# A linear-attention and mixture-of-experts kernel: first 128 tokens as one block without state, first half sequence projected in fp32 from undivided operands

## The chip, the cores and the metric

The kernel runs on one core of a Trainium2 chip. The metric is the device time of one launch in microseconds (us). The kernel before takes 321.5 us (median of three runs, 321.44 to 322.52).

A core has five engines with queues of their own: TensorE (PE) multiplies matrices, with its weight loads shown as PEld; VectorE (DVE) and ScalarE (ACT) work elementwise and read its results; GpSimd (POOL) works elementwise; SyncE (SP) issues the DMAs here. Engines wait for each other by semaphores, and each works through its own queue in order.

## The reference

Two parts follow each other, for 4 sequences of 768 tokens. The first is a gated linear attention with 8 heads of 48 channels:

```
f = 1 / (1 + exp(-f_logit))
for t in range(768):
    state = f[t][:, None] * state + k[t] (outer) v[t]      # per head, 48 x 48
    y[t] = q[t] @ state
x = y of all heads side by side                            # 768 x 384 per sequence
```

The second is a mixture of 4 attention experts with width 64, causal, of which each token takes the best 2 by the logits `x @ w_gate`:

```
q, k, v = x @ wq[e], x @ wk[e], x @ wv[e]
a = softmax(causal(q @ k.T / 8))
out += (weight of e for the token, 0 if not in its top 2) * (a @ v @ wo[e])
```

## The kernel before, in words

**Windows.** The linear attention goes by windows of 128 tokens (`gla_window`), six for each sequence, 24 in all. A window loads f, k, q (names `fkq`) and v. ScalarE makes the logs of the gates, VectorE sums them up along the tokens (a scan, into `c`, L441), ScalarE exponentiates the sums both ways (L447, L448), and VectorE multiplies k by the one (L451) and q by the other (L452). TensorE transposes k (L460), so that it can form the growth of the state, k times v, for each half window of 64 tokens (L485). VectorE adds that to the state (`mid` after the first half, `state` after the second, L501, L504, L506). The scores k times q are made for the two 64-token halves apart (L554), and what a half takes from tokens before it comes from the state (L544). VectorE copies the scores under a causal mask (`copy_predicated`, into `xs`, L564), TensorE multiplies them by v (L579), and the result goes into `x`.

The products on fp32 data in the second part are made from halves: a value is rounded to a reduced form (fp32r), the rest is a second number, and three products (high by high, high by low, low by high: L645, L646, L647 in `mm3`) stand for one. So x has a high half (L295) and a low half (L613), and so have the weights (`weights`: load L372, high L376 or L295, low L381).

**Filling of x.** TensorE works on 128 rows in this kernel, and 8 heads of 48 are three times 128: heads 6 and 7 are spread over spare rows by six small DMAs in each group (`fill`, L300). Window 0 is an exception (`whole`): its products write all 128 rows at once, with the tiles `vz` and `mz` that hold the spread columns of v and of the state.

**Units.** The second part goes by units of half a sequence (384 tokens), eight in all. A unit projects q and k (`proj_qk`, names `qs` and `kk`) and v with the gate logits (`proj_v`, `vv` and `lg`), ranks the logits (`gate`), and for each expert makes scores, maxima (L799, L803), exponentials (L814), divides (L842, L297), transposes (L860), multiplies by v (L890) and by wo. Unit 0 is projected in pieces of 128 tokens, as each of the first three windows is done; the others in pieces of 384.

**Order.** A table of numbers (`SEQUENCE`) names every step in the order in which it is emitted, and a plus behind a number picks another of the engines that can do it. What stands earlier on an engine is done earlier there. A planner (`Order.run`) walks the table to place filler products: products on zeros (`zb`, L274) that keep TensorE busy where the planner expects it to wait; `SURE`, `EARLY` and `LANDS` are numbers of that planner. Weight blocks are loaded into a buffer (`stage`) that is later used for probabilities.

Of the kernel before, what the change touches and what calls it, by code (L numbers as in the profile page):

```python
# [7 lines left out]
F32 = mybir.dt.float32  # L8
# [11 lines left out]
E, HD = 4, 64  # L20
# [22 lines left out]
SURE, EARLY = 1.6, 17.6e3  # L43
# [13 lines left out]
LANDS = (1300, 3.7, 500, 900)  # L57

IN_TURN = ("x", "xs", "qs", "kk", "vv", "lg", "zz", "pt0", "pt1")
# [90 lines left out]
"""  # L150


# [1030 lines left out]
```

## Time and profile before

| | |
|---|---|
| median of 3 runs | 321.5 us |
| profiled execution, device time | 321.65 us |
| its span in the profile | 319.9 us |
| TensorE busy | 304.7 us (95%) |
| VectorE busy | 263.4 us (82%) |
| ScalarE busy | 224.5 us (70%) |
| GpSimd busy | 52.4 us (16%) |
| instructions | 12988 |

The profile is of one execution. Its times count from the start of the span. A product's busy time reaches from its start to the modelled end of its passage, so that neighbours overlap: how fast products follow each other is read from the distance of their starts. A fp32 product appears as two records.

### The profile page before, as it was taken

To read this page: it belongs to the slowest core of one execution; us is meant where nothing else is said; L and a number is where in the kernel's file an instruction comes from. 1 tells how busy PE (TensorE), PEld (TensorE's weight loads), DVE (VectorE), ACT (ScalarE), POOL (GpSimd) and SP (SyncE) were. 2 spreads that over 40 slices of the span, in tenths; PEclk is the share of its full clock that TensorE was granted. 3 is DMA by queue.
4 is the path that set the end of the run, shared out by engine and by line. 5 is a ranking of instruction groups with operands and counts; after the bars stand their busy time and mean duration, and the time that the engine had idled before them with its cause. 6 is when DMAs were issued, how large, how long until landed. Compare 5 with 4: busy or idle time off the path is not lost.

```text
span 319.9 us, 12988 instructions
## 1 busy us (share of the span) xinstructions
PE 304.7 (95%) x5495; PEld 251.9 (79%) x5495; DVE 263.4 (82%) x676; ACT 224.5 (70%) x584; POOL 52.4 (16%) x94
## 2 busy tenths in 40 slices
PE   8989998899999999999999999999998999999992
PEld 3669987698898966998889796888887786997771
DVE  5768889989998986898999996999977794889730
ACT  6546668687978796667988866578977662677740
POOL 6111002110242122010133150000010020102300
PEclk9999999999999999999999999999999999999998
DMA  7955653615404405532613405446300003001202
GB/s 196 240 135 163 160 165 88 178 50 171 96 3 115 130 13 141 160 94 54 184 51 115 114 4 151 139 115 180 95 4 2 28 2 77 11 28 51 76 1 84
DMA packets 14561, 30.90 MB, mean 97 GB/s; under 512 B 2240, under 2 KB 10752, under 8 KB 14496
## 3 DMA queue, kind: packets, MB, share of 16 engines
q1 hardware_dynamic: 14496, 30.00, 33.6%
q8 instruction: 45, 0.74, 1.0%
q14 instruction: 20, 0.16, 0.2%
HBM read 23.01 MB, written 4.72 MB: 87 GB/s over the span
## 4 chain that ended last, share of the span: by engine, by line
PE 60%; DVE 22%; ACT 9%; DMA 3%; issue 3%; SPq 1%; POOL 1%; ACTq 0%; POOLq 0%
PE mm L645 9%; PE mm L890 7%; PE mm L647 7%; PE mm L646 7%; PE sps L782 7%; PE mm L860 5%; PE mm L274 3%; ACT pp L814 3%; DVE nm L799 3%; PE sps L554 3%; PE sps L579 3%; DVE c L441 2%; DVE nm L803 2%; PE mm L485 2%; DVE xs L564 2%
## 5 line engine op out<-in xcount | busy, mean ns | idle before, releaser
L814 ACT ACTIVATE pp<-sps,nm 128x128 f32<-128x128 f32 (+5 forms) x96 | 60.2, 633 | 17.0 <-DVE nm L803 12.1
L842 POOL TENSOR_SCALAR pp<-pp,den,one 128x768 f32<-128x768 f32 (+5 forms) x46 | 38.6, 845 | 149.3 <-DVE den L823 84.0
L295 ACT ACTIVATE pt<-mm 128x384 f32<-128x384 f32 (+4 forms) x94 | 39.0, 450 | 13.9 <-PE mm L860 13.4
L782 PE MATMUL sps<-kk,qs 64*128 64x384 f32 (+4 forms) x384 | 43.4, 340 | 1.3 <-ACT pp L814 1.2
L645 PE MATMUL mm<-x,wqk 128*128 128x384 f32 (+1 forms) x120 | 40.2, 335 | 0.0
L890 PE MATMUL mm<-pt,vv 128*64 128x384 f32 (+2 forms) x304 | 39.3, 406 | 0.1
L646 PE MATMUL mm<-x,wqk 128*128 128x384 f32 (+1 forms) x120 | 38.3, 319 | 0.0
L647 PE MATMUL mm<-x,wqk 128*128 128x384 f32 (+1 forms) x120 | 38.3, 319 | 0.0
L860 PE MATMUL mm<-ident,pp 64*128 64x64 f32 x672 | 34.5, 231 | 1.9 <-POOL pp L842 0.8
L860 PEld LDWEIGHTS mm<-ident,pp 64*128 64x128 f32 x672 | 27.0, 139 | 9.4 <-issue 3.3
L890 PEld LDWEIGHTS mm<-pt,vv 128*64 128x64 f32 x304 | 20.3, 137 | 16.9 <-issue 12.7
L441 DVE TENSOR_TENSOR_SCAN c<-keep,fkq 112x512 f32<-112x512 f32 x24 | 29.5, 1229 | 5.0 <-ACT fkq L436 4.8
L782 PEld LDWEIGHTS sps<-kk,qs 64*128 64x128 f32 x384 | 31.1, 187 | 2.7 <-ACT pp L814 1.5
L803 DVE TENSOR_REDUCE nm<-sps 128x2 f32<-128x768 f32 (+3 forms) x32 | 25.6, 816 | 6.0 <-PE sps L787 4.5
L799 DVE TENSOR_REDUCE nm<-sps 128x1 f32<-128x640 f32 (+1 forms) x32 | 27.4, 884 | 3.4 <-PE sps L787 3.3
L645 PEld LDWEIGHTS mm<-x,wqk 128*128 128x128 f32 x120 | 22.6, 188 | 1.8 <-ACT pt L295 0.2
L645 PE MATMUL mm<-wvg,x 128*128 128x260 f32 x72 | 22.0, 306 | 1.3 <-DMA x<-x 1.3
L647 PEld LDWEIGHTS mm<-x,wqk 128*128 128x128 f32 x120 | 22.7, 189 | 0.0
L646 PEld LDWEIGHTS mm<-x,wqk 128*128 128x128 f32 x120 | 22.7, 189 | 0.0
L445 POOL TENSOR_SCALAR cmax<-c 112x4 f32<-112x4 f32 x24 | 6.7, 281 | 95.3 <-DVE c L441 94.2
L297 ACT ACTIVATE pp<-pp,den 128x256 f32<-128x256 f32 (+5 forms) x31 | 19.6, 638 | 3.1 <-DVE den L823 3.0
L646 PE MATMUL mm<-wvg,x 128*128 128x260 f32 x72 | 20.4, 283 | 0.0
(127 smaller groups left out, 728.9 us busy)
## 6 DMA issues: line engine op xcount, KB each, us to landing
fkq<-fkq SPq DMA_DIRECT2D x21, 672.0 KB, 5.2
v<-v SPq DMA_DIRECT2D x24, 200.0 KB, 5.2
out<-o SPq DMA_DIRECT2D x24, 192.0 KB, 2.6
fkq<-fkq SPq DMA_DIRECT2D x9, 224.0 KB, 6.7
x<-x SPq DMA_DIRECT2D x42, 48.0 KB, 2.5
pt<-wqk SPq DMA_DIRECT2D x3, 256.0 KB, 6.2
pt<-wvg SPq DMA_DIRECT2D x3, 130.0 KB, 4.8
pt<-wo SPq DMA_DIRECT2D x2, 192.0 KB, 3.7
```

The source lines that it names most:

```text
L295: nc.scalar.activation(out, in_, AF.Copy)
L441: nc.vector.tensor_tensor_scan(cb.t.rearrange("r p t -> r (p t)"), self.keep.rearrange("r p t -> r (p t)"), part(0).rearrange("r p t -> r ...
L645: nc.tensor.matmul(ps, lh, rh, start=first, stop=False)
L646: nc.tensor.matmul(ps, lh, rl, start=False, stop=False)
L647: nc.tensor.matmul(ps, ll, rh, start=False, stop=last)
L782: nc.tensor.matmul(out, qs.t[r, lq, tq], kk.t[r, lk, s0:s1], start=x == 0, stop=x == 2 and not diag)
L799: ms = [o.add("max", [("V", dcopy(n))], lambda _, j=j, n=n: nc.vector.tensor_reduce(nm.t[:, 0, j:j + 1], banks[j].t[:, :, :n // 2], axis=A ...
L803: ms = [o.add("max", [("V", dcopy(2 * n))], lambda _, x=x, c0=c0, n=n: nc.vector.tensor_reduce(nm.t[:, x], banks[0].t[:, :, c0:c0 + n], ax ...
L814: nc.scalar.activation(out, in_, AF.Exp, bias=nm.t[:, x, j:j + 1], accum_out=den.t[:, x, j:j + 1])
L842: nc.gpsimd.tensor_scalar(p, p, by, self.one, op0=ALU.mult, op1=ALU.mult)
L860: nc.tensor.transpose(tp.t[:, c:c + 64], pp.t[r, c0 + k * 128:c0 + k * 128 + 128], self.ident[r, r])
L890: nc.tensor.matmul(z.t[64 * j:64 * j + 64, a - p0:p1 - p0], ts[sb // TH]["vv"].t[:, sb % TH, e * HD:(e + 1) * HD], pt.t[:, sb, j, a:p1], s ...
```

## The change

The first window is done as one block of 128 tokens with no state: the scores of all 128 tokens with each other are made (the block of the second half against the first by eight more products), masked into a zeroed triangle (`tri`, in a buffer that later holds probabilities), and multiplied by v in 128 columns. The state products for this window, the zeroing products (`wipe`) and the tile `mz` go. The state itself is still formed, for the next window.

The first three windows write x undivided, in fp32, and the first unit's q, k, v and gate logits are one fp32 product each instead of three (`plain`), from the weights as they were loaded (`raw`). The split weights are needed from unit 1 on. The gate logits stay in the tile of v. The table is another one, and so are the planner's numbers.

```diff
-SURE, EARLY = 1.6, 17.6e3
+SURE, EARLY = 0.0, 0.0
-LANDS = (1300, 3.7, 500, 900)
+LANDS = (1300, 4.1, 300, 300)
 SEQUENCE = """
-0 18 4 35 39 5 61 1 7 9 40 2 3 36 6 67 68 8 37 62 11 12 13 14 42 10 15 63 38 16 20+ 69 44 19+ 17 71 21 46 22 72 41
+19 0 35 66 1 4 2 39 5 3 60 6 7 9 8 10 11 20 70 12 13 40 14 37 36 38 67 22 21 222 42 44 15 57 41 69 63 46 16 18+ 17
...
         if whole:
-            def wipe(e):
-                for c in range(2):
-                    nc.tensor.matmul(ab.t[:, c, NP * C:], self.zb[:, 0:128], self.zb[:, 0:NP * C], start=True, stop=True)
...
+            blank = o.add("st", [("P", 1150)], lambda e: nc.gpsimd.memset(tri(), 0.0), alloc=[full])
...
-            inter(1)
-        t = o.add("a", [("PE", 850 if whole else 760 if w else 747)], scores, [k1, q1, sm, sdone] + ([clear, zm] if whole else []),
+            if not whole:
+                inter(1)
+                return
+            for p in range(NP):
+                for j in range(2):
+                    a = (NP + p) * C
+                    nc.tensor.matmul(ab.t[0:64, 1 - j, a:a + C], part(1)[64 * j:64 * j + 48, p, 0:C],
+                                     part(2)[64 * j:64 * j + 48, p, C:W], start=True, stop=True)
+        t = o.add("a", [("PE", 930 if whole else 760 if w else 747)], scores, [k1, q1] + ([] if whole else [sm, sdone]),
...
         if whole:
+            sel = [o.add("gev", [("V", dcopy(512))], lambda e, k=k, r=slice(64 * k, 64 * k + 64): pred(
+                tri()[r, :, :, k], r, ab.t[r, :, 0:NP * C], self.below[r]), [t, blank], uses=[ab, full]) for k in range(2)]
+            sel.append(o.add("gev", [("A", acopy(512))], lambda e: self.copy(
+                e, tri()[0:64, :, :, 1], ab.t[0:64, :, NP * C:].rearrange("s c (p t) -> s c p t", t=C)), [t, blank], uses=[ab, full]))
...
+            if n < 3:
+                self.windows[n] = o.add("x", [("A", acopy(k)), ("V", dcopy(k))], lambda e: self.copy(
+                    e, xout(0).bitcast(F32), yin()), [y], uses=[ys if whole else ab, x])
...
+                    if plain:
+                        nc.tensor.matmul(ps.t[:, :n], self.raw(1, i)[:, ws], x.t[:, 0, i, cs].bitcast(F32), start=i == 0,
+                                         stop=i == 2)
+                        continue
...
-                        self.proj_qk(o, t, pr, x, a, e, need + wqk)
+                        self.proj_qk(o, t, pr, x, a, e, need + ql, plain=True)
                     for k in ws:
-                        self.proj_v(o, t, x, k, need + wvg)
+                        self.proj_v(o, t, x, k, need + vl, plain=True)
...
-                need += self.fill(o, x, 0, HALF, need)
+                need += self.fill(o, x, 0, HALF, need) + (wqk + wvg if u == 1 else [])
```

What the new table does to the engines' queues is shown at three places. The first is SP's queue from its start, before. `fkq ... 112x512` is one of f, k and q of a window (224 KB), `112x1536` all three (672 KB), `v` 200 KB, `pt_143<-wqk` a block of the q and k weights (256 KB), `pt_143<-wvg` one of the value and gate weights (130 KB). The loads of windows 0 to 2 come singly; the first two are f of windows 0 and 1, and k and q of window 0 come behind the weight block.

```order
L423 DMA fkq<-fkq 112x512 x2
L372 DMA pt_143<-wqk 128x512
L423 DMA fkq<-fkq 112x512 x2
L430 DMA v<-v 128x400
L423 DMA fkq<-fkq 112x512 x4
L430 DMA v<-v 128x400
L423 DMA fkq<-fkq 112x512
L372 DMA pt_143<-wqk 128x512 x2
L430 DMA v<-v 128x400
L428 DMA fkq<-fkq 112x1536
L372 DMA pt_143<-wvg 128x260 x2
```

And now (the names are the same but for the buffer's number):

```order
L432 DMA fkq<-fkq 112x512 x5
L439 DMA v<-v 128x400
L375 DMA pt_146<-wqk 128x512
L432 DMA fkq<-fkq 112x512 x2
L439 DMA v<-v 128x400
L432 DMA fkq<-fkq 112x512
L437 DMA fkq<-fkq 112x1536
L375 DMA pt_146<-wqk 128x512
L439 DMA v<-v 128x400
L375 DMA pt_146<-wqk 128x512
L432 DMA fkq<-fkq 112x512
L375 DMA pt_146<-wvg 128x260 x3
```

The first five loads are now f of windows 0, 1 and 2 and then k and q of window 0. The whole load of window 3 has moved ahead of two weight blocks and of the queries of window 2.

The second place is VectorE's queue, from the key product of window 0 to the masked copy of window 1's scores, before. L451 and L452 are the key and query products, L441 the scan (in the program a `SCALAR_TENSOR_TENSOR`), L564 the masked copy of scores, L613 the low half of x, L381 the low half of weights.

```order
L451 TENSOR_TENSOR fkq<-fkq 112x512
L441 SCALAR_TENSOR_TENSOR c<-keep,fkq 112x512
L452 TENSOR_TENSOR fkq<-fkq,c 112x512
L381 TENSOR_TENSOR wqk<-pt_143,wqk 128x512
L504 TENSOR_TENSOR state<-mm,mid 112x208
...
L506 TENSOR_TENSOR state<-state,c 112x192
L564 COPY_PREDICATED xs_93<-below,sps 128x512
...
L501 TENSOR_TENSOR mid<-mm,state 112x208
...
L613 TENSOR_TENSOR x<-sps,x 128x2x3x64
L564 COPY_PREDICATED xs_94<-below,sps 128x512
```

And now, over the same stretch (L460, L461: the products; L450: the scan; L572: the masked copy; L295: an eviction of transposed keys):

```order
L460 TENSOR_TENSOR fkq<-fkq 112x512
L461 TENSOR_TENSOR fkq<-fkq,c 112x512
L450 SCALAR_TENSOR_TENSOR c<-keep,fkq 112x512
L572 COPY_PREDICATED pt_128<-below,sps 64x8x64 x2
...
L513 TENSOR_TENSOR state<-mm,mid 112x208
L515 TENSOR_TENSOR state<-state,c 112x192
L295 COPY kt<-mm 128x4x64
...
L510 TENSOR_TENSOR mid<-mm,state 112x208
...
L572 COPY_PREDICATED xs_94<-below,sps 128x512
```

The query product stands ahead of the scan, the masked copy is two copies of 64 rows, no split of weights and no low half of x stands in the stretch, and an eviction has come from ScalarE.

The third place is TensorE's queue around window 0's scores, before. L274 are fillers, L554 the scores, L544 and L539 the state's part.

```order
L485 MATMUL mm<-v,kt 48x64
L274 LDWEIGHTS zb
L274 MATMUL sps<-zb 128x256
...
L554 MATMUL sps<-fkq 64x64 x16
L544 MATMUL sps<-fkq,mid 48x64 x3
L539 MATMUL sps<-fkq,mz 64x64 x3
```

And now (L469: transposes of keys; L556 and L565: scores, the second of the new block; L494: state growth):

```order
L469 MATMUL mm<-ident,fkq 128x48
L278 LDWEIGHTS zb
L278 MATMUL sps<-zb 128x512
L556 MATMUL sps<-fkq 64x64 x16
L565 MATMUL sps<-fkq 64x64 x8
L494 MATMUL mm<-v,kt 64x48
```

The scores of window 0 stand ahead of its state growth instead of behind it, and nothing of the state is multiplied for them.

## Rows read from the trace of the kernel before

**Rows 1.** Page, busy time of each engine: us, share of the span, instructions.
```profile
PE 304.7 (95%) x5495; PEld 251.9 (79%) x5495; DVE 263.4 (82%) x676; ACT 224.5 (70%) x584; POOL 52.4 (16%) x94
```

**Rows 2.** Page, chain that ended last, shares of the span by engine.
```profile
PE 60%; DVE 22%; ACT 9%; DMA 3%; issue 3%; SPq 1%; POOL 1%; ACTq 0%; POOLq 0%
```

**Rows 3.** Stages: us, each engine's busy us (instructions), clock, DMA share, GB/s.
```profile
8.00:14.00 6.00, 6.00 (x106) 3.62 (x104) 4.12 (x7) 2.98 (x9) 1.16 (x1) 1.00 1.06 259
16.00:18.00 2.00, 2.00 (x67) 1.64 (x65) 0.55 (x1) 1.12 (x2) 1.14 (x2) 1.00 0.00 0
24.33:45.75 21.42, 21.36 (x503) 19.97 (x501) 18.22 (x43) 13.95 (x35) 1.37 (x5) 1.00 0.54 154
45.75:80.00 34.25, 31.25 (x709) 26.94 (x709) 31.87 (x88) 26.22 (x80) 4.35 (x10) 1.00 0.45 128
80.00:300.00 220.00, 216.41 (x3776) 182.31 (x3776) 191.00 (x500) 163.61 (x424) 37.06 (x53) 1.00 0.29 80
```

**Rows 4.** Chain in order of time, 0 to 50 us: start, us, what.
```profile
1.87 7.96 PE mm L274 x25
...
13.01 0.62 PE sps L554 x32
...
19.98 0.75 DVE xs L564
...
21.58 0.62 PE sps L579 x29
...
23.00 0.72 issue
23.72 0.68 PE mm L485 x25
24.40 0.26 PE mm L645
...
38.06 4.98 DMA fkq<-fkq
...
44.84 1.23 DVE c L441
...
48.08 1.20 DVE nm L803 x2
```

**Rows 5.** Timeline of VectorE, 0 to 26 us: start, us, instruction [idle before].
```profile
7.87 0.69 DVE L451 TENSOR_TENSOR fkq<-fkq 112x512 f32<-112x512 f32 x1 [1.49 <-DMA fkq<-fkq]
...
12.73 0.68 DVE L451 TENSOR_TENSOR fkq<-fkq 112x512 f32<-112x512 f32 x1
...
18.11 0.38 DVE L501 TENSOR_TENSOR mid<-mm,state 112x208 f32<-112x208 f32 x1 [1.56 <-PE mm L485]
...
19.00 0.55 DVE L613 TENSOR_TENSOR x<-sps,x 128x384 fp32r<-128x384 f32 x1
...
20.88 1.34 DVE L381 TENSOR_TENSOR wqk<-pt,wqk 128x512 fp32r<-128x512 f32 x2
```

**Rows 6.** Timeline of TensorE's weight loads, 6 to 10 us.
```profile
6.79 2.55 PEld L274 LDWEIGHTS <-zb 128*128 128x128 bf16 x12 [0.28 <-issue]
```

**Rows 7.** Groups by line and shape: count | busy us, mean ns | idle before.
```profile
L645 PE MATMUL mm<-x,wqk 128*128 128x128 f32 x36 | 10.2, 284 | 0.0
...
L646 PEld LDWEIGHTS mm<-x,wqk 128*128 128x128 f32 x120 | 22.7, 189 | 0.0
```

**Rows 8.** Timeline of TensorE around 24.5 and 42.6 us.
```profile
24.49 0.28 PE L646 MATMUL mm<-x,wqk 128*128 128x128 f32 x1
24.60 0.28 PE L647 MATMUL mm<-x,wqk 128*128 128x128 f32 x1
...
42.55 0.28 PE L647 MATMUL mm<-wvg,x 128*128 128x260 f32 x1
42.67 0.29 PE L645 MATMUL mm<-wvg,x 128*128 128x260 f32 x1
```

**Rows 9.** Chain: probabilities times values of a second-half unit.
```profile
301.03 3.38 PE mm L890 x24
```

More of the change, by code (lines that the diff above doesn't have):

```diff
@@ L219, in run @@
                         t.clear = at
+            for b in t.uses if e in "VA" else ():
+                if b.psum and "VA"[e == "V"] in b.read:
+                    o = "VA"[e == "V"]
+                    start = max(start, b.read[o] + SEEN[o][e])
             start = max(start, free[e] + (leave if e == "PE" and t.modes[0] != mode else 0.0))
@@ L244, in run @@
                 b.left -= 1
+                b.read[e] = t.done
                 for k in b.free_at:
@@ L363, in weights @@
                          (self.wo, self.wo_d, E // 2, DM))[which]
-        last = []
+        last, loads = [], []
         for i in range(n):
@@ L383, in weights, with raw @@
             t = o.add("wl", [("S", 470)], load, alloc=[st], size=cols / 2)
+            loads.append(t)
             t = o.add("w", [("P", 160 + 0.833 * cols), ("A", acopy(cols) + 30)], hi, [t], uses=[st])
             last.append(o.add("w", [("V", dcopy(cols))], lo, [t], uses=[st], port=True))
-        return last
+        return last, loads
+    def raw(self, which, i):
+        a, cols = ((0, 260), (780, 512))[which]
+        return self.raws.t.rearrange("s k q t -> s (k q t)")[:, a + i * cols:a + (i + 1) * cols]
     def gla_pools(self, ctx):
@@ L536, in inter @@
                     g = j ^ (p // 2)
-                    if whole and c and p == 3:
-                        for i in range(3):
-                            nc.tensor.matmul(yo(i, g, c, 64), self.mz[64 * j:64 * j + 48, i],
-                                             part(2)[64 * j:64 * j + 48, p, c * C:c * C + C],
-                                             start=False, stop=cross == 0, skip_group_check=True)
-                    elif w or c:
+                    if w or c:
                         st, m = mid if c else old, outer(g)
@@ L545, in inter @@
                                          part(2)[64 * j:64 * j + 48, p, c * C:c * C + C],
-                                         start=cross == 1 and (g, c) not in begun and not whole, stop=cross == 0, skip_group_check=True)
+                                         start=cross == 1 and (g, c) not in begun, stop=cross == 0, skip_group_check=True)
                         begun.add((g, c))
@@ new lines, in gla_window @@
+            sel.append(o.add("gev", [("A", acopy(512))], lambda e: self.copy(
+                e, tri()[0:64, :, :, 1], ab.t[0:64, :, NP * C:].rearrange("s c (p t) -> s c p t", t=C)), [t, blank], uses=[ab, full]))
+        else:
+            sel = [o.add("gev", [("V", dcopy(512))], lambda e: pred(xsb.t, slice(0, 128), ab.t[:, :, 0:NP * C], self.below),
+                         [t], alloc=[xsb], uses=[ab])]
+        def outputs(e):
+            if whole:
+                for p in range(NP - 1):
+                    for q in (NP - 1, p):
+                        for g in range(2):
+                            v0, m = (2 * p + g) * D, 64 if q > p else 48
+                            nc.tensor.matmul(ys.t[64 * g:64 * g + m, p * W:p * W + W],
+                                             self.vz[:, g, p] if q > p else vb.t[:, v0:v0 + m],
+                                             tri()[:, 1 - (g ^ (q // 2)), q], start=q > p, stop=q == p,
+                                             skip_group_check=True)
+                return
@@ L589, in xout @@
         def xout(h):
-            return x.t[0:rows, h, 0:np_, oc].rearrange("r p (c t) -> r c p t", c=2)
+            out = x.t[0:rows, h, 0:np_, oc]
+            return out if whole else out.rearrange("r p (c t) -> r c p t", c=2)
         def yin():
-            return ab.t[0:rows, :, NP * C:(NP + np_) * C].rearrange("r c (p t) -> r c p t", p=np_)
+            if whole:
+                return ys.t[:, 0:np_ * W].rearrange("r (p t) -> r p t", p=np_)
+            return ab.t[:112, :, NP * C:].rearrange("r c (p t) -> r c p t", p=np_)
         place = o.place
@@ L604, in go @@
                     more(e)
-            y = o.add("y", [("PE", 760 + 310 * whole + cost)], go, [sel, lv] + ([zv] if whole else []) + list(needs),
-                      alloc=alloc,
-                      uses=[xsb, vb, fkq, x, mid, ab] + ([old] if w else []) + list(uses), modes=("q", "q"), edge=(0, 92))
-            y.spare, y.free = lambda: [ab.t[0:112, i, NP * C:] for i in range(0 if w else 1, 2)], t
-            k = np_ * W
+            y = o.add("y", [("PE", 1290 if whole else 760 + cost)], go, sel + [lv] + ([zv] if whole else []) + list(needs),
+                      alloc=list(alloc) + ([ys] if whole else []),
+                      uses=[vb, x] + ([full] if whole else [xsb, fkq, mid, ab]) + ([old] if w else []) + list(uses),
+                      modes=("c", "c") if whole else ("q", "q"), edge=(60, 100) if whole else (0, 92))
+            if not whole:
+                y.spare, y.free = lambda: [ab.t[0:112, i, NP * C:] for i in range(0 if w else 1, 2)], t
+            k = np_ * W
+            if n < 3:
+                self.windows[n] = o.add("x", [("A", acopy(k)), ("V", dcopy(k))], lambda e: self.copy(
+                    e, xout(0).bitcast(F32), yin()), [y], uses=[ys if whole else ab, x])
+                o.place = here
+                return y
             hi = o.add("x", [("A", acopy(k)), ("V", dcopy(k))], lambda e: self.copy(e, xout(0), yin()),
-                       [y], uses=[ab, x])
+                       [y], uses=[ys if whole else ab, x])
             self.windows[n] = o.add("x", [("V", dcopy(k))], lambda e: nc.vector.tensor_sub(xout(1), yin(), xout(0)),
-                                    [hi], uses=[ab, x])
+                                    [hi], uses=[ys if whole else ab, x])
             o.place = here
@@ L620, in gla_window, with fill @@
         return state[:2] + (None, finish)
-    def fill(self, o, x, a, b, needs):
+    def fill(self, o, x, a, b, needs, halves=2):
         out = []
@@ L629, in go @@
                 def go(e, i=i, r=r):
-                    self.move(x.t[r + 48:r + 64, :, i, a:b], x.t[r + 16 * i:r + 16 * i + 16, :, 3, a:b])
-                out.append(o.add("fill", [("S", 640)], go, needs, uses=[x], size=(b - a) / 8))
+                    self.move(x.t[r + 48:r + 64, 0:halves, i, a:b], x.t[r + 16 * i:r + 16 * i + 16, 0:halves, 3, a:b])
+                out.append(o.add("fill", [("S", 640)], go, needs, uses=[x], size=(b - a) / 16 * halves))
         return out
@@ L1072, in plan @@
                     o.place = 12.0 + 4 * k
[L1073 removed]
+                    fills[k] = self.fill(o, x, 128 * k, 128 * k + 128, [windows[k]], 1) if k else []
                 for a, e, ws in ((0, 128, (0,)), (128, 256, (1,)), (256, 384, (2,))):
```

86 lines of the change are left out of this document (41 added, 45 removed), and 107 rows, old and new, of the table SEQUENCE.

## The prediction

> **What bounds the kernel now.** First the page's table of engines: TensorE is busy for 95% of the span and VectorE for 82% [rows 1]. The chain that ended last is not TensorE alone, since 22% of it lies on VectorE [rows 2]. So I cut the span into stages [rows 3]. From 24.33 to 45.75 us, where the first half sequence is projected while the attention windows 3 to 5 are computed between, TensorE works 21.36 of 21.42 us and VectorE 18.22. From 45.75 to 80 TensorE has gaps of 3.0 us in 34.25 and VectorE works 31.87: there VectorE is as near to being the bound. From 80 to 300 TensorE is busy for 98%. What is saved before 45.75 is therefore kept, if the stages behind it start earlier by as much and get no more work.
>
> Before 24.33 nothing is full: TensorE's 22.07 us are partly the filler products on zeros (25 of them in one run of 7.96 us [rows 4]). This is a chain of waits, and the chain of work in order of time shows it [rows 4]: scores of window 0 at 13.01, the masked copy of window 1's scores at 19.98, its output products at 21.58, the last state product at 23.72, and the first projection at 24.40. Behind it VectorE's timeline [rows 5]: the key product of window 0 waits for its DMA until 7.87, that of window 1 comes at 12.73, the low half of x of window 0 at 19.00 and two low halves of weights end at 22.22. Meanwhile the DMA engines moved nothing from 16 to 18 us [rows 3], because the fourth window's load stood at the head of SP's queue and waited for a buffer.
>
> **The head, step by step.** Times are my estimates, laid out by hand from the durations in the rows.
> 1. Window 0's keys are still the fourth load: f of window 2 (224 KB) has taken the place of a weight block (256 KB) ahead of them. So the key product stays at 7.8 (0.69 long). The filler ahead of the transposes shrinks from two short products and 25 to 21; late ones are 0.21 apart (twelve in 2.55 [rows 6]), so TensorE is free at about 8.5 and the transposes start at 8.7, not after the 1.3 us of filler that now lies between.
> 2. Scores of window 0 no longer need the state, its two copies, or the wiping products: they wait for two VectorE products alone. The query product now stands ahead of the scan: 7.8 + two of 0.65 = 9.1, scores from 9.3 to 10.3 (24 products, where 16 take 0.62). Today 13.01 to 13.63.
> 3. Scan of window 1 (1.23 [rows 4]) to 10.4; then two masked copies of 64 rows at 0.75 each, since a copy's time goes by columns, not rows: to 11.9. That is one copy more than before.
> 4. Window 1's keys: with them 2024 KB are queued, 1096 more than with window 0's keys today, which landed at 7.87. At the 259 KB/us of the stretch from 8 to 14 us [rows 3] that is 4.2 us later: about 12.0. Its key product runs 12.0 to 12.7, today 12.73 to 13.41.
> 5. Behind it on VectorE: a scan (1.2), two products (1.3), an eviction and three state operations (0.3 to 0.4 each), the wait for ScalarE's exponential (0.5): window 1's masked copy at about 17.5, today 19.98. The low half of x (0.55), one masked copy and the wait for a state sum that stands before 18.11 [rows 5] are what goes.
> 6. Output products of window 1 at 18.4, today 21.58; last state product at 19.4, today 23.72 (before it stood 0.72 us of a stall of TensorE's own [rows 4], which I let go); first projection at 20.2, today 24.40: **4.2 us**.
>
> The projection's other inputs are in time: it needs raw weights, not split ones, so it waits for a DMA alone. By the same count the last of the three q and k blocks, 3832 KB into the queue, lands at 7.87 + 2904 / 259 = 19.1, give or take 1. This is the tightest point: if it slips past 20.2, each us costs one.
>
> **The projections of the first half.** Removed: 36 products of 128 columns, three times [rows 7], 0.11 apart [rows 8]: 108 x 0.111 = 12.0 us; and 27 of 260 columns, 0.12 apart with switching 0.13: 3.5. Added: 36 fp32 products of 128 columns and 9 of 260. The nearest fp32 row is the product of probabilities and values [rows 9]: 1920 columns for two column halves at once (four times 384, 256, 128) in 3.38, or 1.76 ns per column. That gives 0.225 and 0.458 each: 8.1 + 4.1 = 12.2. **Saving 3.3 us**, and all of it in a stage where TensorE is full. Bounds: if a tenth of the row is start-up (an estimate), 1.6 ns per column and 11.1; if every product also had to wait for two weight loads at 0.11 each, 45 x 0.22 = 9.9 more, 22.1. I take 12.2, as the row is the same kind of product.
>
> A rule of the Trainium skill speaks against this part (FP8 and Floating Point Precision, section TensorE Precision Notes): true fp32 is four passes through the array, where three products of the reduced form are three. By that ratio the projections would take 15.5 x 4/3 = 20.7 instead of 12.2 and the whole 323.2. The trace disagrees for 128 columns: reduced products of 128 columns follow each other as slowly (0.11) as nearly those of 260 (0.12) [rows 8], so half of their time is not columns, and the fp32 row has no such share. For 260 columns the two come out alike: 0.458 against 0.37.
>
> **Smaller things.** The low halves of x for three windows (0.55 for the first [rows 5], the others a little longer) go, about 1.8 us of VectorE; the small copies of gate logits, which join the evictions of values, I count as nothing. Against that, two splits of the q and k weights (0.67 each [rows 5]) and three of the value weights (half as wide, so 0.35) move from before 45.75 into or past the experts' start, where VectorE is near the bound. The blanking of the triangle (1024 columns) is on GpSimd, idle there. The fill DMAs keep their number (0.6 us of SP each) and halve their bytes, nothing on the path. I charge **0.6 us** for VectorE's displaced work, between 0 and 1.5.
>
> **Is it kept?** The chain today passes the load of window 6: issued 38.06, scan 44.84, first maxima 48.1 [rows 4]. It is issued when window 3's outputs are done; four fifths of the way from the first projection to the first scores, which takes 21.4 us today and, less the saving up to there (nine of the twelve q and k products and all of v: 2.5), 18.9: near 32.2, and the scan near 39. VectorE's list from window 2's query product (near 21) to the first maxima adds up to some 18.5 us by the durations above, so 40 without a wait, 41 to 42 with. Both gain 6 to 7 us: neither takes the place of TensorE's gain.
>
> **Sum.** The profiled execution took 321.65, of which the span is 319.9; the median is 321.5. 321.65 - 4.2 - 3.3 + 0.6 = 314.75; against the median 314.6. I say **314.7**, own range 312.3 to 317.3. The rest of the order table is redone too; where the order says the same work, I give it no gain or loss, and 1.5 us either way in that range.
>
> **Rivals.**
> - *Weight loads are not hidden (slower).* Place: TensorE from 20 to 40 us, all 45 fp32 products. An fp32 product with 128 stationary columns does not appear in this trace; rows 9 load 64. If both loads lay bare, 22.1 replaces 15.5: +6.6, less 4.2 of the head, and the displaced 0.6: 324.6. It decides from a mean of 0.44 us per product: (15.5 + 4.2) / 45. Against it: the reduced products come 0.11 apart although a load takes 0.19 [rows 7, 8], so loads already run beside products on the same rows. The rule that a load overlaps only with products on other rows of the array (TensorE: Matmul & The Clock Gate, Part 3: Packing small matmuls) would give this case; the trace disagrees with it there.
> - *The head does not move, the queue takes it back.* The 672 KB load of window 3 now stands ahead of two weight blocks and window 2's queries on SP, and waits for window 0's buffer. If that wait lasts to 13.6 as the scores do now, the last block lands at 22 to 23 and 2.5 us of the 4.2 go: 317.2; with a missed cover for windows 4 and 5 also, 319. For it: that wait is real today (the silent 16 to 18 us). Against: the buffer is now free without the output products.
> - *Same time.* VectorE from 45.75 to 80 is the bound and the new table is worse there by as much as is won: it holds 31.87 of 34.25 us; 1.5 us of splits plus some 5 us of worse interleaving give 321. Against: VectorE has only 2.4 us of gaps there today, and the stage before gives it 1.3 us less to do.
> - *More is won.* The relieved VectorE closes half of TensorE's 3.0 us of gaps between 45.75 and 80 and the splits cost nothing: 312 or less.
>
> **Numbers.** Own case 0.62; queue 0.16 (317.2 to 319.9); more 0.08; same 0.06; slower 0.08. What a measurement here can tell from no change is 0.5%, 1.6 us: faster is below 319.9, slower above 323.1. Faster 0.85, same 0.07, slower 0.08. The range runs from 312 to 319.9: it leaves out the slower and same cases and part of the faster tail.
>
> **What would show it.** Right: first projection near 20 us (19.5 to 21), its fp32 products 0.22 apart for 128 columns (the records come in two halves, 0.11 apart), first expert scores near 39, first maxima 40 to 42, then a span that keeps some 7 us. Wrong: products 0.44 apart; a wait for a weight DMA before the first projection; VectorE idle before the maxima with TensorE's gaps growing between 40 and 75 us; or a head as predicted and a gain that shrinks between 45 and 300 us.

## The result, and the profile after

The changed kernel takes 310.96 us (median of 4, 310.47 to 313.43), the kernel before beside it 322.01 (median of 4): 0.967 of the time, 95% interval 0.962 to 0.972. A second series of six gave 310.37. Beside that series and the three that ran with it (e5 to e8) nine of the fourteen executions of the kernel before that the ratios rest on had a granted clock of only 0.974 to 0.984 (median 324.1 instead of 321.6), so those four ratios come out some 0.008 too low, and versions are compared below by their times. The forecast was 314.7, with 312.0 to 319.9 as its range: the direction was right, and 11 us were gained where 7 were expected. The first profiled execution of the changed kernel took 313.43, its span 311.6; the second series' took 310.98, its span 309.2.

Engines on the page after [rows 1]:

```profile
PE 298.1 (96%) x5399; PEld 245.4 (79%) x5399; DVE 263.0 (84%) x652; ACT 221.5 (71%) x577; POOL 53.3 (17%) x99
```

TensorE lost 6.6 us of busy time, VectorE 0.4. The stages, with the columns of [rows 3]:

```profile
8.00:14.00 6.00, 5.90 (x118) 3.61 (x118) 5.27 (x9) 3.42 (x11) 0.78 (x2) 1.00 1.01 258
16.00:18.00 2.00, 1.53 (x58) 1.24 (x57) 1.92 (x5) 1.54 (x4) 0.00 (x0) 1.00 1.07 329
20.08:39.96 19.88, 19.70 (x465) 16.89 (x464) 18.08 (x46) 12.53 (x34) 2.33 (x5) 1.00 0.57 154
45.00:80.00 35.00, 32.58 (x675) 27.16 (x677) 31.64 (x83) 27.02 (x78) 5.66 (x11) 0.90 0.39 107
80.00:300.00 220.00, 217.83 (x3806) 182.19 (x3804) 192.05 (x479) 163.94 (x426) 38.19 (x58) 1.00 0.28 79
```

The DMA engines, silent from 16 to 18 us before, now move 329 GB/s there. From 45 to 80 us stands something that no stage of before has: the granted clock (TensorE's clock as a share of its full speed) is 0.90. Behind 80 us TensorE is busy for 99% (before 98%).

The head on TensorE's timeline, with the first projections and the first expert scores [rows 4, 8]:

```profile
8.72 0.46 PE L469 MATMUL mm<-ident,fkq 64*128 64x64 f32 x8
...
9.61 0.69 PE L556 MATMUL sps<-fkq 48*64 48x64 f32 x32
...
18.54 0.69 PE L599 MATMUL sps<-xs,v 64*64 64x64 f32 x32
...
19.25 0.67 PE L494 MATMUL mm<-v,kt 64*48 64x48 f32 x32
...
20.08 2.17 PE L698 MATMUL mm<-x,pt 128*128 128x128 f32 x18
...
25.22 1.58 PE L733 MATMUL mm<-pt,x 128*128 128x260 f32 x6
...
39.96 0.79 PE L821 MATMUL sps<-kk,qs 64*128 64x384 f32 x6
```

and on VectorE's [rows 5]:

```profile
7.72 0.69 DVE L460 TENSOR_TENSOR fkq<-fkq 112x512 f32<-112x512 f32 x1 [1.36 <-ACT c L457]
...
12.27 0.69 DVE L460 TENSOR_TENSOR fkq<-fkq 112x512 f32<-112x512 f32 x1
...
17.22 0.73 DVE L572 COPY_PREDICATED xs<-below,sps 128x512 f32<-128x512 uint32 x1
...
41.83 1.26 DVE L842 TENSOR_REDUCE nm<-sps 128x2 f32<-128x256 f32 x2
```

Scores of window 0 at 9.61 (forecast 9.3), window 1's keys at 12.27 (12.0), its masked copy at 17.22 (17.5), its output products at 18.54 (18.4), the last state product at 19.25 (19.4), the first projection at 20.08 (20.2), the first maxima at 41.83 (40 to 42). An fp32 product leaves two records: 18 of 128 columns take 2.17 us, the last of them some 0.28, so 1.89 / 17 = 0.111 per record and 0.222 per product (0.225); six of 260 columns give (1.58 - 0.39) / 5 x 2 = 0.476 (0.458). Every step of the head lies within half a us of the forecast; the first expert scores, at 39.96, are one us behind the 39 that was forecast, and the maxima are in their range. So the head does not hold the 4 us that were gained beyond the forecast.

To find them, I take a landmark that is the same work in every version, the last product of unit 1's values and gates, and with it TensorE's last product. Before:

```profile
73.62 0.28 PE L647 MATMUL mm<-wvg,x 128*128 128x260 f32 x1
...
313.42 0.34 PE L647 MATMUL mm<-wo,zz 128*128 128x384 f32 x1
```

The changed kernel, second series:

```profile
67.57 0.28 PE L677 MATMUL mm<-wvg,x 128*128 128x260 f32 x1
...
302.49 0.34 PE L677 MATMUL mm<-wo,zz 128*128 128x384 f32 x1
```

Ahead of the landmark 6.05 us are gained, behind it 4.88 (239.80 becomes 234.92), where the forecast had nothing. In the first profiled execution the landmark stands at 69.90 and the rest takes 235.08: the two executions differ ahead of it, by 2.3 us, and hardly behind it.

### The profile page after: what moved, and what is told of

Read it like the earlier page. It is cut to its first block, busy times and chain, and to the rows that moved or that the text cites. A ratio compares the mean times of both kernels' runs of the same rounds, so it can differ in the third digit from the quotient of the medians.

```text
span 311.6 us, 12756 instructions
## 1 busy us (share of the span) xinstructions
PE 298.1 (96%) x5399; PEld 245.4 (79%) x5399; DVE 263.0 (84%) x652; ACT 221.5 (71%) x577; POOL 53.3 (17%) x99
## 5 line engine op out<-in xcount | busy, mean ns | idle before, releaser
L853 ACT ACTIVATE pp<-sps,nm 128x384 f32<-128x384 f32 (+5 forms) x96 | 60.2, 633 | 17.1 <-DVE nm L842 12.4
L881 POOL TENSOR_SCALAR pp<-pp,den,one 128x384 f32<-128x384 f32 (+5 forms) x50 | 39.4, 797 | 145.8 <-DVE den L862 82.6
L299 ACT ACTIVATE pt<-mm 128x384 f32<-128x384 f32 (+4 forms) x91 | 37.6, 443 | 15.2 <-PE mm L899 14.7
L450 DVE TENSOR_TENSOR_SCAN c<-keep,fkq 112x512 f32<-112x512 f32 x24 | 29.6, 1232 | 2.1 <-ACT fkq L445 1.3
L675 PE MATMUL mm<-x,wqk 128*128 128x384 f32 x84 | 29.7, 354 | 0.7 <-ACT o L299 0.4
L842 DVE TENSOR_REDUCE nm<-sps 128x2 f32<-128x256 f32 (+3 forms) x32 | 25.4, 813 | 3.6 <-PE sps L826 3.4
L677 PE MATMUL mm<-x,wqk 128*128 128x384 f32 x84 | 28.3, 337 | 0.0
L676 PE MATMUL mm<-x,wqk 128*128 128x384 f32 x84 | 28.3, 336 | 0.0
L295 DVE COPY pt<-mm 128x384 f32<-128x384 f32 (+4 forms) x39 | 19.0, 500 | 2.8 <-PE mm L899 2.8
L456 ACT ACTIVATE fkq<-c 112x512 f32<-112x512 f32 x24 | 15.1, 629 | 6.3 <-DVE c L450 6.3
L853 ACT ACTIVATION_READ_ACCUMULATOR pp<-sps,nm 128x1 f32 x96 | 19.4, 202 | 0.0
L675 PE MATMUL mm<-wvg,x 128*128 128x260 f32 x63 | 19.1, 303 | 0.1
L546 PE MATMUL sps<-fkq,mid 48*48 48x64 f32 (+1 forms) x368 | 18.9, 219 | 0.0
```

Source lines behind the costliest of these rows:

```text
L299: nc.scalar.activation(out, in_, AF.Copy)
L450: nc.vector.tensor_tensor_scan(cb.t.rearrange("r p t -> r (p t)"), self.keep.rearrange("r p t -> r (p t)"), part(0).rearrange("r p t -> r ...
L675: nc.tensor.matmul(ps, lh, rh, start=first, stop=False)
L676: nc.tensor.matmul(ps, lh, rl, start=False, stop=False)
L677: nc.tensor.matmul(ps, ll, rh, start=False, stop=last)
L842: ms = [o.add("max", [("V", dcopy(2 * n))], lambda _, x=x, c0=c0, n=n: nc.vector.tensor_reduce(nm.t[:, x], banks[0].t[:, :, c0:c0 + n], ax ...
```

## The experiments

Times are medians; each ratio, with its 95% interval, is against the kernel before, run beside it. "Ahead" is the start of the landmark in the profiled execution, "behind" the time from there to TensorE's last product. Behind the landmark executions of the same order agree within 0.4 us (234.71 to 235.08); medians of the unedited changed kernel differ by 0.6 (310.37 and 310.96), so a difference of that size between two series says nothing.

**Whose gain is the order's?** e1 is the changed code with the old order behind the gate of unit 1; e2 is the reverse, before's code with the new order from there on. The edit of e1 where the two orders part (pieces of two lines of the table; in e2 the same, the other way round):

```diff
-308 305 456 205+ 199 309 206+ 198 192 567 ...
+... 308 305 192 193 205+ 198 306 206+ 456 457 ...
...
```

> The changed kernel, but from the ranking of unit 1's gate logits on (about 75 us) every step stands in the order of the table before; nothing is left out. If the 4 us that were not forecast come from the new order of the later steps, this loses them: 314.5 to 316. If they come from work that VectorE no longer has (24 small logit copies), or from the head, the order does nothing and it stays at 310.5 to 311.5.

> The kernel before with its own head and operations, but from the ranking of unit 1's gate logits on in the order of the new table (the 21 logit copies that only it has stand right behind the evictions of values). If the later order is worth 4 us by itself: 317 to 318.5, and the saving grows between 80 and 300 us. If the gain hangs on VectorE's relief or on the head: 321 to 322.

e1 takes 315.42, 0.981 (0.971 to 0.991), as expected if the later order makes the gain. Its landmark stands at 67.61, and behind it are 239.11:

```profile
67.61 0.28 PE L688 MATMUL mm<-wvg,x 128*128 128x260 f32 x1
...
306.72 0.34 PE L688 MATMUL mm<-wo,zz 128*128 128x384 f32 x1
```

e2 takes 320.32, 0.996 (0.993 to 0.998), between its two expectations and nearer to the second. Behind its landmark are 239.49:

```profile
72.58 0.28 PE L658 MATMUL mm<-wvg,x 128*128 128x260 f32 x1
...
312.07 0.34 PE L658 MATMUL mm<-wo,zz 128*128 128x384 f32 x1
```

So the new order is worth 4.2 us behind the landmark with the changed code (239.11 to 234.92), and 0.3 with the code of before (239.80 to 239.49). The changed code alone is worth 0.7 there. Each of the two by itself is next to nothing; together they are 4.9.

**Where along the way?** e6 is the changed kernel with the old order from unit 3's gate on only.

> The changed kernel with the order of the kernel before from the gate of unit 3 on (about 141 us), where the run with the old order from unit 1's gate on (about 75 us) was 4.4 us slower than the changed kernel. Theory A, the new order gains evenly all along: two thirds of the 4.4 us are lost, 314. Theory B, the gain is made between 75 and 141 us, where the lead over the kernel before shrinks from 4.1 to 2 us and which is a matter of the two halves of the second sequence: nothing is lost, 311. Theory C, all of it is made behind 141 us, where the lead grows again: 315.4.

e6 takes 321.47, 0.992 (0.988 to 0.996): worse than any expectation, and no answer. At the seam of the two orders the planner sees waits, and behind 75 us the trace has 26 filler products where that of e1 has 5. The run tells of the seam. Its start is the changed kernel's, and is used below.

**What in the code does the new order need?** Behind unit 1's gate the codes differ in the way the gate logits leave PSUM, the memory into which TensorE writes its results. Now they leave with the values, in one eviction (a copy out of PSUM) of 260 columns; before, VectorE copied the 4 columns of logits by themselves, 24 times, from the same bank (piece of PSUM) as the values. e9 puts the copies back into the changed kernel, right behind the evictions of values (with the tile `lg` and its readers, not shown); e10 joins the two evictions in e2.

```diff
-        t["v done"].append(o.add("hev", [("A", acopy(260)), ("V", dcopy(260))], ... ps.t[:, 0:260] ...
+        t["v done"].append(o.add("hev", [("A", acopy(256)), ("V", dcopy(256))], ... ps.t[:, 0:256] ...
+        t["l done"].append(o.add("hev", [("V", 79)], lambda e: nc.vector.tensor_copy(lg.t[:, ti], ps.t[:, 256:260]),
```

> The changed kernel and its order, but the four gate logits of each of the 24 token blocks are again taken out of PSUM by a VectorE copy of their own (0.08 us by the planner, 24 of them) right behind the copy of the values. Theory A, the joined eviction is what lets the new order gain 4.2 us behind 67 us where it gains 0.3 with the code of before: 313 to 315. Theory B, the small copies cost their own time at most: 311 to 312 (24 x 0.08 = 1.9 us on an engine that is busy for 85%). Theory C, they hide in VectorE's waits: 310.9.

> The kernel before with the new order from unit 1's gate on (that run gave 320.3) and, added to it, the joined eviction of values and logits as in the changed kernel, in all units. Theory A, the joined eviction and the new order need each other: the 4.2 us that the order gains in the changed kernel come out here too, 316 to 317. Theory B, they are independent: 319.5 to 320.3.

e9 takes 316.54, 0.982 (0.977 to 0.988), and is 5.4 to 6.2 us slower than the changed kernel: more than any theory expected, A included (313 to 315). Behind its landmark are 238.55. e10 takes 316.90, 0.985 (0.981 to 0.988), is 3.4 us faster than e2, as theory A expected, and has 236.19 behind its landmark:

```profile
70.10 0.28 PE L689 MATMUL mm<-wvg,x 128*128 128x260 f32 x1
...
308.65 0.34 PE L689 MATMUL mm<-wo,zz 128*128 128x384 f32 x1
```

```profile
73.81 0.28 PE L657 MATMUL mm<-wvg,x 128*128 128x260 f32 x1
...
310.00 0.34 PE L657 MATMUL mm<-wo,zz 128*128 128x384 f32 x1
```

So the joined eviction is what the new order needs, in both directions. It is not quite all: e10 keeps 1.3 us more behind the landmark than the changed kernel (236.19 against 234.92), and no run says why. What the copies cost is seen in their groups by line: count | busy, mean ns | idle time of the engine ahead of them and what ended it. Before, the copies of the logits and the evictions of values that are on ScalarE:

```profile
L295 ACT ACTIVATE vv<-mm 128x256 f32<-128x256 f32 x15 | 5.8, 385 | 7.2 <-DVE lg L703 6.6 <-PE mm L647 0.6
L703 DVE COPY lg<-mm 128x4 f32<-128x4 f32 x24 | 3.6, 153 | 1.9 <-ACT vv L295 1.5 <-PE mm L647 0.3
```

e2 and e9:

```profile
L714 DVE COPY lg<-mm 128x4 f32<-128x4 f32 x24 | 3.7, 156 | 4.8 <-ACT vv L306 4.7
L756 DVE COPY lg<-mm 128x4 f32<-128x4 f32 x24 | 3.6, 155 | 6.1 <-ACT vv L311 6.1
```

Before, it is mostly ScalarE that waits, 6.6 us for the copies, 5.2 of them behind the landmark; VectorE's 1.9 us all lie ahead of the landmark (1.35 of them in one wait that ends at 44.76 us), and behind it its 19 copies do not wait at all. In the new order 17 of the 24 value evictions are on ScalarE instead of 15, and in e9 VectorE stands idle for 6.1 us until ScalarE has read the same bank: 2.4 ahead of the landmark, where e9 is 2.5 behind e5, the second series of the changed kernel, and 3.7 behind it, where 3.6 are lost. In e2 3.5 of the 4.8 us lie behind the landmark, and joining the evictions gains 3.3 there (239.49 to 236.19). So with before's code the new order brings VectorE, which is busy for 82%, waits of about the size of what it would win, which fits the 0.3 that it is worth there. In the trace it is ScalarE's semaphore that releases the copy. One of them, ScalarE's row and VectorE's:

```profile
69.05 0.39 ACT L311 ACTIVATE vv<-mm 128x256 f32<-128x256 f32 x1 [0.65 <-PE mm L689]
```

```profile
69.47 0.16 DVE L756 COPY lg<-mm 128x4 f32<-128x4 f32 x1 [0.28 <-ACT vv L311]
```

ScalarE ends at 69.44, the copy starts at 69.47, and what is queued behind it on VectorE is late by the wait. Is it the copies' own time that costs, or the wait? e13 keeps all 24 copies of e9 and gives each to the engine that evicts the values (in the table a plus marks the 7 that stay on VectorE).

```diff
-        t["l done"].append(o.add("hev", [("V", 79)], lambda e: nc.vector.tensor_copy(lg.t[:, ti], ps.t[:, 256:260]),
+        t["l done"].append(o.add("hev", [("A", 150), ("V", 79)], lambda e: self.copy(e, lg.t[:, ti], ps.t[:, 256:260]),
```

> As the run with the 24 separate copies of the gate logits in the new order (316.5), but each copy goes to the engine that evicts the values of the same block (17 to ScalarE, 7 stay on VectorE), so none waits for another engine's reading of the same bank. Theory A, what costs is VectorE standing in front of the copies (6.1 us in that profile): most of the 5.6 us comes back, 311 to 312.5. Theory B, the copies' own time on the engines counts wherever they are: 314 or more.

e13 takes 310.71, 0.963 (0.958 to 0.967), a little less than theory A expected, and has 234.71 behind the landmark:

```profile
68.92 0.28 PE L689 MATMUL mm<-wvg,x 128*128 128x260 f32 x1
...
303.63 0.34 PE L689 MATMUL mm<-wo,zz 128*128 128x384 f32 x1
```

Its groups of copies:

```profile
L311 ACT ACTIVATE lg<-mm 128x4 f32<-128x4 f32 x17 | 3.0, 177 | 0.0
L307 DVE COPY lg<-mm 128x4 f32<-128x4 f32 x7 | 1.1, 150 | 0.0
```

The same copies, 4.1 us busy, cost nothing that can be measured. e13 takes the own time of 17 copies off VectorE along with the waits (17 x 0.155 = 2.6 us), so it does not part the two by itself. But 2.6 is less than half of what e9 lost, and in the old order all of the copies' time and waits together are worth 0.7 at most behind the landmark (before against e1), while the waits have the size of the loss in e9 and e2. What cost in the new order was, for the most part, VectorE's wait for ScalarE, with VectorE's list behind it.

**What are the head and the projections worth?** Fillers are put into the changed kernel: in e3 20 of 0.21 us ahead of the first projection, in e4 one in each of the 15 projection groups of the first half, and in e7 the same with the old order of e1. First the edit of e3, then that of e4 and e7, for q and k and for v.

```diff
-            def product(e, ps=ps, ws=ws):
+            def product(e, ps=ps, ws=ws, m=m):
+                for _ in range(20 if plain and first and m and not pr else 0):
+                    nc.tensor.matmul(ps.t, self.zb[:, 0:128], self.zb, start=True, stop=True)
```

```diff
             def product(e, ps=ps, ws=ws):
+                if plain:
+                    nc.tensor.matmul(ps.t, self.zb[:, 0:128], self.zb, start=True, stop=True)
...
         def product(e):
+            if plain:
+                nc.tensor.matmul(ps.t, self.zb[:, 0:128], self.zb, start=True, stop=True)
```

> The changed kernel with 20 filler products on zeros (0.21 us each) right before the first projection, so that it starts at about 24.4 us as before the change. If the head's 4.3 us are kept to the end: 315 to 315.6. If TensorE's start is not what decides behind it (VectorE or the loads are): 311 to 313.

> The changed kernel with one filler product (0.21 us) ahead of each of the 15 projection groups of unit 0, together 3.2 us of TensorE, what the fp32 projections were reckoned to save. If that stage is bound by TensorE: 313.8 to 314.5. If VectorE hides it: 311 to 312.

> The changed kernel with the old order from unit 1's gate on and one filler product of zeros (0.21 us) in each of the 15 projections of the first half sequence, 3.2 us of TensorE in all. In the changed kernel itself these fillers cost only 0.3 us. Theory A, what the projections save is hidden by waits before 75 us whatever stands behind: no slower than the old order alone, 315.4 to 315.8. Theory B, the projections' saving is kept in full and it was the new order that took the fillers up again: 318.6.

e3 takes 315.42, 0.981 (0.974 to 0.988): about 4.5 us are lost where 4.2 were put in. e4 takes 311.26, 0.967 (0.962 to 0.972): 0.3 lost of 3.2. e7 takes 315.44, 0.973 (0.968 to 0.979): against e1's 315.42, from another series, nothing is lost of 3.2. So the head is kept whole, and in these kernels the faster products bring next to nothing, whatever order stands behind. The reason is in 45 to 60 us. The changed kernel is repeated without an edit (e5); columns as above:

> The changed kernel once more, unedited, for comparison beside the next three. Both theories: 0.966 to 0.969 of the kernel before. What it is to tell besides is the spread: if the drop of TensorE's granted clock behind 51 us (0.50 for some 6 us in the execution profiled first) comes in only some of the executions, their times should fall into two lots, about 310.6 and 312 to 313.5; if it comes in all, they lie together.

```profile
45.00:51.00 6.00, 3.98 (x138) 3.25 (x138) 5.93 (x15) 5.86 (x20) 2.81 (x6) 1.00 0.37 115
51.00:55.00 4.00, 4.00 (x54) 2.36 (x46) 2.79 (x7) 0.85 (x2) 0.00 (x0) 0.57 0.35 64
55.00:60.00 5.00, 5.00 (x110) 4.68 (x108) 4.71 (x9) 4.41 (x14) 0.56 (x1) 1.00 0.60 156
```

e5 takes 310.37, 0.955 (0.950 to 0.961), its six executions 308.65 to 311.18. They do part, though not at the times that were expected: 308.65 and 308.87 have a granted clock of 0.996 and 0.997 over the whole execution, the other four (309.77 to 311.18) 0.990 to 0.992. From 45 to 51 us VectorE is the bound (5.93 of 6.00), TensorE stands still for 2.0, and then it runs at a granted 0.57 for 4 us, near the lower of its two levels, 1.2 of 2.4 GHz (in the first profiled execution 0.55 for 4 us, then 0.68 for 5; in e13 0.50, the lower level itself, for 4 us). Such a drop takes 0.006 off the clock of the whole execution (an estimate: 4 x 0.43 / 309), so at 0.996 and 0.997 there was none of that size, and in this series it costs some 2 us; in the first series the execution at 0.997 is no faster than the rest (311.15). In e4 and e7 the granted clock is 1.00 from 45 to 80 us. The faster projections bring TensorE to VectorE's queue sooner, where it waits, and in most executions it then runs slow: of six profiles in which nothing is put in ahead of 60 us (both of the changed kernel, e1, e6, e9, e13) five show the drop. The one without is e6, with the same gaps:

```profile
45.00:51.00 6.00, 3.95 (x143) 3.31 (x144) 5.93 (x14) 5.97 (x20) 2.80 (x6) 1.00 0.39 121
51.00:55.00 4.00, 4.00 (x102) 3.12 (x96) 3.98 (x10) 2.44 (x7) 0.00 (x0) 1.00 0.35 64
```

Its landmark:

```profile
65.80 0.28 PE L688 MATMUL mm<-wvg,x 128*128 128x260 f32 x1
```

e5 and e1, with the drop, have it at 67.57 and 67.61: the drop costs 1.8 us there (in the first profiled execution, with the longer drop, the landmark at 69.90 is 4.1 behind). e8 lays eight filler outputs into the gaps; e14 keeps only the three of `("tr", 0, 0)`. The edit of e8:

```diff
         t.pad = max(0, int((start - max(at, 3000) - CHANGE) / FILL_COST + SURE * (start < EARLY)))
+        t.pad += {("a", 1, 2): 1, ("s", 0, 1): 1, ("y", 1, 2): 1, ("tr", 0, 0): 3, ("tr", 0, 2): 1}.get(t.key, 0)
```

> The changed kernel with eight filler products of zeros (0.21 us each, 1.7 in all) laid into waits of TensorE between 43 and 51 us, where it stood still for 2.5 us before its granted clock fell to 0.50. Theory A, the fall of the clock comes from these gaps and costs what the profile shows (some 6 us at half clock, 2 to 2.5 us of the time): no drop behind 51 us in this trace, 310.3 or less, and a narrow spread. Theory B, the drop is made up by slack behind it: 310.5 to 311. Theory C, the fillers stand in the way of work that is ready: up to 1.7 us slower, 312.7.

> The changed kernel with only three filler products (of the eight of the earlier run, 309.4), all of them in the longest wait between 43 and 51 us, ahead of the first transposes of the probabilities. Theory A, what drops the clock is the longest waits: no drop, 309 to 309.4, since the five others cost TensorE something. Theory B, it is the sum of the scattered gaps: the drop behind 51 us stays in this trace, 310.4 to 311.

e8 takes 309.40 (309.16 to 310.87), 0.955 (0.950 to 0.960):

```profile
45.00:51.00 6.00, 5.11 (x128) 3.88 (x130) 5.86 (x17) 5.87 (x19) 2.79 (x6) 1.00 0.36 109
51.00:55.00 4.00, 4.00 (x88) 3.02 (x84) 4.00 (x10) 2.54 (x8) 0.00 (x0) 1.00 0.44 87
55.00:60.00 5.00, 5.00 (x142) 4.63 (x138) 4.96 (x10) 4.41 (x15) 0.56 (x1) 1.00 0.65 184
```

There is no drop; the landmark comes at 66.45, between e6 and e5 (the fillers take some of it back), and behind it 234.98 is unchanged. Since e6 has no drop either, one trace doesn't prove that the fillers held the clock; the six executions of e8, which lie within 1.7 us, agree with it. e14 takes 310.31 (309.51 to 313.14), 0.963 (0.957 to 0.968): there is no drop in its trace either (1.00 from 45 to 60 us), but its median is the changed kernel's, so it fits neither theory. e8 has the lowest median here, 1.0 us below the changed kernel beside it. It beats the kernel before; that it beats the changed one is not shown, since the ranges overlap and the two executions of e5 without the drop are faster than any of e8.

The same two prices are taken once more without the drop: e11 is e8 with e3's fillers, e12 is e8 with e4's.

> The kernel with the eight fillers between 43 and 51 us (309.4, no drop of the clock) and 20 filler products of 0.21 us (4.2 us) right ahead of the first projection, so that the projections start where they did before. It prices the head without the drop of the clock. If all of the head's 4.2 us are kept: 313.6. If VectorE is the bound from 45 to 60 us (14.8 of 15 us busy) and its list ahead of there does not start later by as much: 311.5 to 312.5. If nothing of it counts: 309.4.

> The same kernel with eight fillers, and one filler product of 0.21 us in each of the 15 projections of the first half sequence (3.2 us). It prices what a faster projection is worth without the drop of the clock. All kept: 312.6. Two thirds, as the profiles without a drop have it so far (unit 1's gate at 73.5 against 71.3 us): 311.6. Nothing: 309.4; then not the clock but VectorE hid the projections' saving.

e11 takes 313.79, 0.978 (0.975 to 0.982): 4.4 us are lost of 4.2. e12 takes 311.82, 0.972 (0.967 to 0.977): 2.4 lost of 3.2, in its profile 1.7 ahead of the landmark (68.12) and 1.1 behind it (236.07). Both had 1.00 from 45 to 80 us. e8 is from another series, so each price is good to some 0.6 us.

## Why the prediction was right in its direction and too small

| term | forecast | measured | from |
|---|---|---|---|
| head | -4.2 | -4.4 | e11 against e8 |
| projections, without the drop | -3.3 | -2.5 | e12 against e8, 2.4 of 3.2 us, times 3.3 |
| VectorE's displaced work | +0.6 | not measured apart | |
| drop of the clock from 51 us | none | +1.0 | e5 against e8, less what e8's fillers cost |
| joined logits and order, behind 67 us | 0 | -4.9 | 239.80 to 234.92 |

From the 321.65 of before's profiled execution: 321.65 - 4.4 - 2.5 + 1.0 - 4.9 = 310.85; e5's profiled execution took 310.98. The terms are not known as well as this agrees: the first two are differences of medians from different series. Ahead of the landmark the forecast had 6.9 and 6.05 were gained; that it was too high there hid part of how much it was too low behind.

- *The head.* Right, step by step; a masked copy takes 0.73 us with 64 rows and 0.74 with 128, as was counted. The rival of the queue did not come: the load of window 3 went out at 10.79 us instead of 17.16, and the first projection shows no wait for a weight block.
- *The projections.* Right in their size: 0.222 and 0.476 per product, so 36 x 0.222 + 9 x 0.476 = 12.3 against the forecast's 12.2. The prediction's other estimates, 20.7 by passes and 0.44 per product with bare weight loads, did not come. Wrong is "all of it in a stage where TensorE is full" as a reason that it is kept: the end of the saving lies in 45 to 51 us, where VectorE bounds. "Both gain 6 to 7 us" was near for VectorE's list (first scores 39.96 against 45.75, maxima 41.83 against 48.08) and too much for the load of window 6, which went out at 33.36 instead of 38.06 with its scan at 40.70 instead of 44.84. (That load is issued 0.64 of the way from the first projection to the first scores, not "four fifths"; the 32.2 is worked out with 0.64.) Behind the maxima VectorE's list had no more room: from 40 to 75 us TensorE's gaps grew from 2.76 us to 3.15 (e5), half of one of the prediction's signs of being wrong (the other half, an idle VectorE ahead of the maxima, did not come), and of the 3.3 us 2.5 are kept without the drop of the clock and 0.3 in the kernel as it is.
- *The step that failed: "where the order says the same work, I give it no gain or loss", with 1.5 us either way.* Behind the landmark the new order gains 4.2 us with the joined evictions (e1 against the changed kernel), more than the miss of 3.7. The other term set to nothing, "the small copies of gate logits, which join the evictions of values, I count as nothing", is right by itself: with the old order the changed code gains 0.7. But it is the condition of the first: with the copies left in, the new order is worth 0.3 (e2), since VectorE then waits for ScalarE. The two were set to nothing apart, and together they are 4.9. The trace of before could not give this price, because behind the landmark its copies do not wait. What it does show is that two engines waited for each other over that bank, 6.6 and 1.5 us, so that the order of the two readings was a thing to price. The code had a sign of it too, which was passed over: the changed planner reckons with an engine that waits for another's reading of a bank (`b.read`), and that of before does not. I priced a worse table at 5 us in a rival and a better one at nothing.
- *Luck.* With the old order behind unit 1's gate e1 takes 315.4, against the forecast 314.7, but that is not the forecast sum come true: in e1 the smaller gain of the projections and the drop of the clock, which the forecast lacked, stand against the charge of 0.6 and the 0.7 of the changed code.
- *"More is won" (0.08).* Its time, 312 or less, came true, and its mechanism not: from 45 to 80 us TensorE's gaps shrank from 3.0 to 2.3 us (e5), not by half, between 45 and 60 they even grew from 1.4 to 2.0, and the gain is behind 67 us. Its own pieces add up to 314.75 - 0.6 - 1.5 = 312.65, not to 312 or less.

What stays open: how the order wins its 4.2 us in the joined kernel. From e1 to e5 no single wait goes. Behind the landmark TensorE's idle time falls by 1.0 us (from 239.11 - 235.95 to 234.92 - 232.76, its busy time there) and its busy time by 3.2. Of these, fillers are 1.1 (5 of them, 1.9 us, become 2, 0.8 us) and the experts' scores with their masks 2.4 (60.2 us to 57.8, with the same products at the same mean length, so that they overlap more); the rest is small. Which places of the order do this was not tested. Nor was the step of VectorE's displaced work priced apart.

## What to carry to other kernels

A removed operation can be worth more than its own time: taking out 24 small copies was worth 0.7 us at most with the old order and 3.4 with the new one. Before writing nothing beside such an operation, ask which engine would wait at that place in the order that is to come, above all where two engines read one PSUM bank; the idle column of the old profile tells of the old order only. When code and order change together, price them together, and price a good order as far from zero as a bad one. A landmark of equal work, read in every version, splits a gain into ahead and behind at the cost of two rows. And a saving on TensorE that ends in front of another engine's queue can be lost twice, as it was in most executions here: as a wait, and in a lower clock that followed it.

## What the hardware showed that was not expected

- *The clock.* TensorE's granted clock fell behind 51 us (to 0.50 to 0.73 from 51 to 55) in five of six profiled executions in which nothing was laid into the waits from 43 to 51 us, and from 45 to 80 us stayed at 1.00 in e6, with the same waits, and in e3, e4, e7, e8, e11, e12 and e14. Gaps alone do not decide: e3 too stood still for 2.5 us between 45 and 55. What does was not found.
- *Two readers of one bank.* The copy of e9 began 0.03 us after ScalarE's read. Here a semaphore orders them, so the runs don't show what the chip would do by itself. The Trainium skill (Advanced Engine Details and Errata, section Bank Collisions) says that TensorE, VectorE and ScalarE cannot access the same PSUM bank within the same partition on the same cycle, and that ScalarE and VectorE can access PSUM at full bandwidth at once if they do not meet in a bank; no run here shows either. e13 shows a cheap way around the wait: one engine for both reads.
- *Small copies.* Four columns of 128 rows take 0.15 us on VectorE, where the planner counts 0.079, and 0.18 on ScalarE (e13).
